# Moving spills and fetches of spectra, and the transposes of normalised rows, around the down projection

## Chip, cores and metric

The kernel runs on one core of a Trainium2 chip. The metric is the device time of one execution in microseconds (us), the median of several runs. The profile is one further execution, recorded by the hardware profiler; its span is a little shorter than the device time, since it starts with the first and ends with the last recorded instruction.

## The reference, cut to what matters

A block of 2048 rows of width 576 goes through an adaptive layer norm with a long causal convolution (part A), and then through another adaptive layer norm with a gated feed-forward network of inner width 4608 (part B). Everything is in bf16.

```python
mod = silu(c) @ w_mod                       # six rows: sa, ca, ga, sb, cb, gb
h = layernorm(q) * (1 + ca) + sa
k_shift = sum over 4 taps of shifted k * shift_k
kv = k_shift * v
y = irfft(rfft(kv padded) * rfft(ssm_k padded))[:S] + kv * ssm_D
x = q + ga * (h * y)
h = layernorm(x) * (1 + cb) + sb
out = x + gb * ((silu(h @ w1) * (h @ w3)) @ w2)
```

## The kernel before, in words

The rows are cut into eight blocks of 256. Part A is a block convolution: for each block s the kernel makes a spectrum X[s] of kv and a spectrum V[s] of the filter, each a tile of 128 x 3456 bf16 (864 KB). The outcome of block s is the sum over j of X[j]*V[s-j], multiplied and added on VectorE (DVE, `pair`, L439 and L441, or L434 for the first term), turned back by matmuls on TensorE (PE, `inverse`, L573), and added to the rows x1 (L587, L588). SBUF holds three X and four V at a time. Older ones are spilled to memory (`keep_x`, L446; `keep_v`, L450) and fetched again when a later block needs them (`get`, L463).

Part B works on pairs of blocks, 512 rows at a time, r = 0 to 3. In the up phase (`stream`, L1018 and L1029; `stream_halves`, L1086, for r = 3) PE multiplies the transposed normalised rows h2T by w1 and w3. In the down phase (`down`, L1143) it multiplies the hidden tile by w2: the output is made in two halves of 288 columns, and each half takes nine pieces of w2 of 288 KB, with 16 matmuls a piece. I number the pieces of one down phase p0 to p17, so p0 to p8 are the first half and p9 to p17 the second. Each piece is loaded by L1132 into one of four buffers, so the load of a piece can be issued when PE has done the piece four before it. These buffers share the memory of the weight tile wst2.

While PE runs row pair r, the convolution of the pair r+1 (blocks 2r+2, even, and 2r+3, odd) runs as a generator beside it: each job and each piece advances the generator by a planned cost (`advance`), and `end()` runs it to its end. Its last steps are, for each of the two blocks, the sums of the layer norm (ScalarE, ACT, L470), its scale (DVE, GpSimd), the normalised rows h2row (ACT, L599), two transposing DMAs from h2row to h2T (`turn_all`, L823), and the scale and shift on the transposed tile (`modulate`, L838 on ACT or L836 on DVE). There is one h2row tile, so the odd block's rows can be written only when the even block's transposes have read it. There are two h2T tiles, for even and odd r.

All these DMAs are issued from SyncE's queue (SP), in one order that the scheduler settles when the program is built: `issue_after(x)` keeps an instruction behind x, and `behind(engine)` behind the newest instruction of that engine. The PSUM pool has four tiles. The down phase's second half holds two of them until DVE has taken them out (`og`, L1168).

In the kernel before, the even block's transposes are issued in the last steps of its own outcome, as soon as its rows are normalised, and are modulated in the next outcome; the odd block's transposes come from `down`, at the eighth piece of the second half (TURN = 7, which is p16), with the modulation behind them. All fetches of old spectra stand behind the last w2 piece of the first half (p8). The spills of X[2] and V[3] stand in the first down phase, that of V[2] in the up phase after it.

Of the kernel before, what the change touches and what calls it, by code (L numbers as in the profile page):

```python
# [24 lines left out]
NRB = S // RB  # L25
FC = 4
NW13 = 3
W2C = 4
# [3 lines left out]
FIRST_DUE = 12.0  # L32
N1 = 24
SPLIT = 2
HEAD = 8
HEAD_PACE = 1.4
AHEAD = 2
EPS = 1e-5
FIRST = (4, 5, 6, 0, 7, 1, 8, 2, 3)
TURN = 7  # L40
QUICK = False


# [6 lines left out]
class _Kernel:  # L50
    def __init__(self, ctx, tc, q, k, v, shift_k, ssm_k, ssm_D, w1, w3, w2, c, w_mod, out):
        self.tc, self.nc = tc, tc.nc
        self.q, self.k, self.v = q, k, v
        self.shift_k, self.ssm_k, self.ssm_D = shift_k, ssm_k, ssm_D
        self.w1, self.w3, self.w2, self.c, self.w_mod, self.out = w1, w3, w2, c, w_mod, out
        pool = lambda name, **kw: ctx.enter_context(tc.tile_pool(name=name, **kw))
        self.const = pool("const", bufs=1)
        self.psum = pool("psum", bufs=4, space=bass.MemoryType.PSUM)
        self.dram = pool("spill", bufs=1, space=bass.MemoryType.DRAM)
        self.spec = pool("spec", bufs=4)  # L60
        self.wprev = pool("wprev", bufs=2)
        self.prod = pool("prod", bufs=1)
        self.acc = pool("acc", bufs=1)
        self.ld = pool("ld", bufs=1)
        self.kvp = pool("kvp", bufs=1)
        self.x1p = pool("x1p", bufs=4)
        self.lnp = pool("lnp", bufs=1)
        self.small = pool("small", bufs=4)
        self.hp = pool("hp", bufs=3)
        self.xo, self.hg, self.accs, self.l1 = {}, {}, {}, {}  # L70
        self.X, self.V, self.Wl = {}, {}, {}
        self.w13, self.kept = {}, {}
        self.last_w2 = None

    def newest(self):
        return self.nc.cur_bb.bb.instructions[-1]
# [382 lines left out]
    def get(self, which, i):  # L459
        t = self.spec.tile([P, 6, D], BF16, name=which, tag=which, bufs=3 if which == "X" else 4)  # L460
        src = self.Xd if which == "X" else self.Vd
        with self.tc.issue_after(self.last_w2) if self.last_w2 is not None else nullcontext():
            self.nc.sync.dma_start(t[:].rearrange("p a d -> p (a d)"), src[i])  # L463
        return t

# [307 lines left out]
    def outcome(self, s, fill, waits, between=None, then=None, quick=False):  # L773


        def steps():
            nc = self.nc
            yield self.real_parts(s)
            yield -waits[0]
            y = self.lnp.tile([P, 2, D], BF16, name="y", tag="y")  # L780
            for cc in range(2):
                nc.scalar.copy(y[:, cc, :].rearrange("p (h d) -> p h d", h=2), self.inverse(s, cc)[:, :, 0:H])
            yield -waits[1]
            self.residual(s, y)
            yield 1.5
            if between is not None:
                between()
            if quick:
                st = []
                for cc in range(2):  # L790
                    st.append(self.quick_stats(self.xo[s][:, cc, :], "l2"))
                    yield 1.25
                for cc in range(2):
                    self.normed(s, cc, *st[cc])
                    yield 0.75
            else:
                sums = [self.small.tile([P, 2], F32, name="l2" + k, tag=t) for k, t in (("s", "ssum"), ("q", "ssq"))]
                for i in range(2):
                    with self.behind(nc.scalar):
                        self.ln_sums(self.xo[s], i, *sums)  # L800
                    yield 0.0
                yield -waits[2] / 2
                if then is not None:
                    then()
                stats = self.ln_var(*sums, "l2")
                yield -waits[2] / 2
                scales = self.ln_shift(*stats)
                yield -3.0
                for cc in range(2):
                    self.normed_act(s, cc, *scales)  # L810
                    yield -1.0
            yield -waits[3]
            self.accs.pop(s)
            self.hg.pop(s)
        yield from self.mix(steps(), fill)

    def turn_all(self, s):

        if s > 1:
            hT = self.h2T[(s // 2) % 2]  # L820
            for cc in range(2):
                t = 2 * (s % 2) + cc
                self.nc.sync.dma_start_transpose(hT[:, :, t * P:(t + 1) * P], self.h2row[:, cc, :])  # L823
            return
        pt = self.ps((P, 2, 1024), BF16)
        for cc in range(2):
            self.turn(pt, cc)
        self.turned(s, pt, 0, 2)

    def modulate(self, s, quick):  # L830

# [30 lines left out]
    def conv(self, s0):  # L862
        s1 = s0 + 1
# [64 lines left out]
        yield from self.mix(self.x_spectrum(s0), beside())  # L928
        yield from self.x_sums(s0)
        yield from self.pair(self.X[s0], V0, s0)  # L930

        def more():
            if not (s0 != 4):
# [2 lines left out]

        def others():
            yield from self.kv_rows(s1)
            self.gate_shift(s1)
            if s0 != 4:  # L940
                yield from self.pair(self.X1, self.V[s0], s1)
            yield from self.mix(self.x_spectrum(s1), more())
            yield from self.x_sums(s1)
        yield from self.outcome(s0, others(), (7.0, 4.5, 6.0, 0.0), lambda: self.gate_rows(s1))
        yield from self.pair(self.X[s1], V0, s1)
        if s1 + 1 < NBLK:
            with self.behind(self.nc.sync):
# [1 line left out]
                self.pair_taps(s1 + 1)  # L949
        yield from self.gate(s1)  # L950
        ahead = self.mix(self.filter_ahead(s1 + 1)) if s1 + 1 < NBLK else ()
        yield from self.outcome(s1, ahead, (5.0, 4.5, 5.0, 0.0), lambda: self.turn_all(s0),
                                lambda: self.modulate(s0, QUICK))

    def filter_ahead(self, s):
        yield -4.0
# [165 lines left out]
    def down(self, r, rate):  # L1122
        nc = self.nc
        for h in range(2):
# [4 lines left out]
            for n, fc in enumerate(FIRST if r == 0 else range(NF // W2C)):  # L1129
                f0 = n * W2C  # L1130
                w = _ap(self.w2m, (h * NF + f0) // W2C % NW2 * W2C * H, [[H, W2C], [1, H]])
                nc.sync.dma_start(w, self.w2[fc * W2C * P:(fc + 1) * W2C * P, h * H:(h + 1) * H]  # L1132
                                  .rearrange("(a p) d -> p a d", p=P))
                last = f0 + W2C == NF
                if h == 0 and last:
                    self.last_w2 = self.newest()
                order = [(f, t) for f in range(W2C) for t in range(4)]
                if f0 == 0:
                    order = [(f, t) for t0 in (0, 2) for f in range(W2C) for t in (t0, t0 + 1)]
                if last:  # L1140
                    order = [(f, t) for t in range(4) for f in range(W2C)]
                for f, t in order:
                    nc.tensor.matmul(acc[t],  # L1143
                                     self.h3[:, fc * W2C + f, t * P:(t + 1) * P], w[:, f, :],
                                     start=(f0 + f == 0), stop=(f0 + f == NF - 1))
                if h == 1 and f0 // W2C == TURN and r + 1 < NRB:

                    self.end()
                    self.turn_all(2 * r + 3)
                    if 2 * r + 5 < NBLK:  # L1150
                        self.pair_taps(2 * r + 5)
                    self.modulate(2 * r + 3, r > 0)
                if (f0 // W2C) % 4 == 3:

                    leave = ((self.keep_v, 3), (), (self.keep_x, 2), (),) if r == 0 else ()
                    for keep, i in filter(None, leave[2 * h + f0 // (4 * W2C):][0:1]):
                        keep(i)
                self.advance(rate * W2C * 4 * 0.126)
            cols = slice(h * H, (h + 1) * H)
            for a in range(2):  # L1160
                s = 2 * r + a
# [41 lines left out]
    def row_blocks(self, n1):  # L1203
        for r in range(NRB):
            cost = 0
            if r + 1 < NRB:
                s0 = 2 * r + 2
# [5 lines left out]
            if r == 0:  # L1213

                jobs = [(fc, 256, 512, None, None) for fc in (n1 - 2, n1 - 1)]

                new = [(n1 + i, 0, RB, b, None) for i, b in enumerate((2, 1, 2))]
                again = [(fc, 256, 512, b, None) for fc, b in enumerate((0, 0, 1, 0))]
                while new or again:
                    jobs += new[0:1] + again[0:1]  # L1220
                    new, again = new[1:], again[1:]
            else:
                spills = {1: (self.keep_x, 1), 2: (self.keep_v, 2), 3: (self.keep_x, 3), 5: (self.keep_v, 0), 6: (self.keep_v, 1)} if r == 1 else {}
                bufs = [b if b == 2 else (r + b) % 2 for b in (0, 1, 2, 0, 1, 2, 0, 1, 0)]
                jobs = [(fc, 0, RB, bufs[fc], (lambda f, i: lambda: f(i))(*spills[fc]) if fc in spills else None)
                        for fc in range(NF // FC)]
# [59 lines left out]
```

## Time and profile before

| | |
|---|---|
| time, median of 3 runs | 504.66 us (504.37 to 505.38) |
| span of the profile | 501.9 us |
| PE busy | 488.2 us, 97% |
| DVE busy | 338.4 us, 67% |
| ACT busy | 282.5 us, 56% |
| DMA queue of SP | 107.4 MB, 71.8% of the 16 DMA engines' span |

The stages can be told apart on PE by the line of its matmuls. The first block and the setup take up to 33 us, the up phase of r = 0 lasts to 122, its down phase to 161, up and down of r = 1 to 277, those of r = 2 to 391, and r = 3 runs to the end. The busy share of an engine over the whole span is a mean over these stages. The profile counts an engine idle before an instruction and names what ended that idle time last[...].

### The profile page before, as it was taken

The numbers are of one execution on the slowest core, as the hardware profiler recorded it, in microseconds if no ns is written. First come the engines' busy times: TensorE is split into PE (matmuls) and PEld (weight loads), VectorE is DVE, ScalarE is ACT, GpSimd is POOL, SyncE is SP. The second block draws the span as 40 slices with busy tenths as digits, with TensorE's granted clock in tenths as the row PEclk, the third lists the DMA queues.
The fourth block names the chain that finished last, engine by engine and source line by source line (L and its number), as shares of the span: only waits on it lengthen the run. The fifth ranks groups of instructions, "written<-read, shape, count | busy, mean of one in ns | idle before, by whom it ended". The sixth has DMA issues, their size and how long they took to land.

```text
span 501.9 us, 8868 instructions
## 1 busy us (share of the span) xinstructions
PE 488.2 (97%) x3528; PEld 286.3 (57%) x3528; DVE 338.4 (67%) x448; ACT 282.5 (56%) x561; POOL 23.0 (5%) x41
## 2 busy tenths in 40 slices
PE   7999999999999999999999999999999999999996
PEld 3667775547776444343777433434777444444774
DVE  8989898898999567997176999699762211111012
ACT  6658679659244688579450456966734355555000
POOL 4200000000001000000000000100000000000000
PEclk9999999999999999999999999999999999999999
DMA  8989986759999878557799897644575454460562
GB/s 281 315 213 235 322 261 204 217 165 313 262 353 304 273 266 247 160 162 223 210 307 340 301 285 247 190 135 148 167 182 136 152 179 148 133 189 1 143 168 67
DMA packets 115037, 107.97 MB, mean 215 GB/s; under 512 B 20340, under 2 KB 107573, under 8 KB 114997
## 3 DMA queue, kind: packets, MB, share of 16 engines
q1 hardware_dynamic: 114974, 107.41, 71.8%
q8 instruction: 27, 0.44, 0.4%
q14 instruction: 14, 0.11, 0.1%
q10 hardware_dynamic: 22, 0.01, 0.0%
HBM read 92.46 MB, written 9.44 MB: 203 GB/s over the span
## 4 chain that ended last, share of the span: by engine, by line
PE 66%; DVE 17%; DMA 8%; ACT 5%; issue 2%; SPq 1%; POOL 0%; POOLq 0%; DVEq 0%; ACTq 0%
PE ps L1018 28%; PE ps L1143 15%; PE ps L1086 14%; PE ps L1029 4%; DMA wst<-in_B_w_dram 4%; DVE p L439 3%; DMA V<-Vd 2%; DVE z L441 2%; ACT junk L470 2%; DVE z L434 2%; DVE og L1168 2%; PE ps L348 2%; DMA kh<-in_A_k_dram 1%; PE ps L573 1%; DVE h L1043 1%
## 5 line engine op out<-in xcount | busy, mean ns | idle before, releaser
L1018 PE MATMUL ps<-h2T,wst 128*128 128x512 bf16 (+1 forms) x1056 | 200.5, 341 | 0.4 <-ACT X L350 0.2
L1018 PEld LDWEIGHTS <-wst 128*128 128x128 bf16 x1056 | 100.1, 98 | 86.7 <-issue 15.0
L1143 PE MATMUL ps<-wst,h 128*128 128x288 bf16 x1152 | 144.9, 286 | 2.2 <-DMA wst<-in_B_w_dram 2.1
L1143 PEld LDWEIGHTS <-h 128*128 128x128 bf16 x1152 | 112.6, 98 | 32.8 <-issue 4.2
L1036 ACT ACTIVATE h<-ps 128x512 bf16<-128x512 f32 x108 | 64.8, 600 | 79.3 <-PE ps L1029 50.3
L1086 PE MATMUL ps<-h2T,wst 64*128 64x512 bf16 x648 | 70.3, 376 | 0.0
L1040 ACT CAST u<-ps 128x512 bf16<-128x512 f32 x108 | 63.3, 586 | 0.0
L439 DVE TENSOR_TENSOR p<-X,V 128x3456 bf16<-128x3456 bf16 x28 | 54.7, 1953 | 4.3 <-DMA V<-Vd 3.9
L441 DVE TENSOR_TENSOR z<-z,p 128x3456 bf16<-128x3456 bf16 x28 | 54.6, 1950 | 0.1
L1086 PEld LDWEIGHTS <-wst 64*128 64x128 bf16 x648 | 31.1, 94 | 38.6 <-DVE og L1168 0.2
L1113 DVE TENSOR_TENSOR h<-h,u 128x1024 bf16<-128x1024 bf16 x18 | 12.5, 692 | 58.1 <-ACT u L1110 58.1
L1043 DVE TENSOR_TENSOR h<-h,u 128x1024 bf16<-128x1024 bf16 x54 | 36.9, 685 | 15.0 <-ACT u L1040 15.0
L1107 ACT ACTIVATE h<-ps 128x512 bf16<-128x512 f32 x36 | 21.5, 597 | 39.8 <-PE ps L1086 39.8
L470 ACT ACTIVATE junk<-x 128x576 bf16<-128x576 bf16 x52 | 35.7, 686 | 3.1 <-DVE x L588 2.6
L1168 DVE TENSOR_TENSOR og<-ps,gbrow 128x576 bf16<-128x576 f32 (+1 forms) x18 | 12.3, 686 | 34.2 <-PE ps L1143 33.6
L1029 PE MATMUL ps<-h2T,wst 64*128 64x512 bf16 (+1 forms) x264 | 33.5, 342 | 0.1
L1110 ACT CAST u<-ps 128x512 bf16<-128x512 f32 x36 | 20.9, 579 | 0.0
L1029 PEld LDWEIGHTS <-wst 64*128 64x128 bf16 x264 | 8.5, 94 | 21.5 <-issue 18.8
L838 ACT ACTIVATE h2T<-h2T,sbcol,cbcol 128x256 bf16<-128x256 bf16 x20 | 10.4, 589 | 16.8 <-DMA h2T<-h2row 16.8
L599 ACT ACTIVATE h2row<-x,l2n,l2r 128x576 bf16<-128x576 bf16 (+1 forms) x24 | 13.8, 654 | 10.2 <-DVE l2n L488 10.2
L368 DVE TENSOR_TENSOR kv<-kv,p 128x1152 bf16<-128x1152 bf16 x24 | 18.1, 753 | 0.3
L362 DVE TENSOR_TENSOR p<-kh,shk 128x3456 bf16<-128x3456 bf16 x8 | 15.6, 1953 | 0.8 <-ACT shk L211 0.6
(135 smaller groups left out, 362.5 us busy)
## 6 DMA issues: line engine op xcount, KB each, us to landing
wst<-in_B_w_dram SPq DMA_DIRECT2D x80, 512.0 KB, 5.1
wst<-in_B_w_dram SPq DMA_DIRECT2D x72, 288.0 KB, 3.4
wst<-in_B_w_dram SPq DMA_DIRECT2D x80, 64.0 KB, 3.3
kh<-in_A_k_dram SPq DMA_DIRECT2D x7, 720.0 KB, 7.0
X<-Xd SPq DMA_DIRECT2D x5, 864.0 KB, 6.8
V<-Vd SPq DMA_DIRECT2D x5, 864.0 KB, 6.0
Xd<-X SPq DMA_DIRECT2D x4, 864.0 KB, 7.7
Vd<-V SPq DMA_DIRECT2D x4, 864.0 KB, 5.5
```

What stands on the lines that cost most here:

```text
L439: nc.vector.tensor_mul(p[:], X[:], V[:])
L441: nc.vector.tensor_add(z[:], z[:], p[:])
L470: self.nc.scalar.activation(junk[:], src[:, i, :], func, scale=scale, accum_out=out[:, col:col + 1])
L1018: nc.tensor.matmul(gus[k][:, i, a * n:(a + 1) * n], w[:, 5 * i + ct, (fi + a) * P:(fi + a + 1) * P], hT[:, ct, t0:t1], start=(first and ct ...
L1029: nc.tensor.matmul(gus[k][:, i, a * n:(a + 1) * n], w[rows, 4, (fi + a) * P:(fi + a + 1) * P], hT[rows, 4, t0:t1], start=(first and a == 0 ...
L1036: nc.scalar.activation(self.h3[:, f:f + m, t0:t1], gus[k][:, 0, :].rearrange("p (a t) -> p a t", a=m), ACT.Silu)
L1040: nc.scalar.copy(self.u[:, k % 2, :], gus[k][:, 1, :])
L1043: nc.vector.tensor_mul(h3, h3, self.u[:].rearrange("p b (a t) -> p (b a) t", a=m))
L1086: nc.tensor.matmul(gus[k][:, i, :], ws[fc][rows, 5 * i + ct if ct < 4 else 4, cols], hT[rows, ct, :], start=swap == 0 and ct == 4, stop=sw ...
L1107: nc.scalar.activation(h3, gus[k][:, 0, :], ACT.Silu)
L1143: nc.tensor.matmul(acc[t], self.h3[:, fc * W2C + f, t * P:(t + 1) * P], w[:, f, :], start=(f0 + f == 0), stop=(f0 + f == NF - 1))
L1168: nc.vector.tensor_mul(g[:, cc, :], ps, _ap(self.gbrow, h * H, [[0, n], [1, H]]))
```

## The change

Four things are changed. The spills of X[2] and V[2] go into the up phase of r = 0, right behind the work that makes them (`keep_v(2)` and `keep_x(2)` in `conv`), instead of the first down phase and the up phase after it. Of the fetches, only the first two (EARLY = 2) that follow a down phase's first half stay behind p8; all later ones stand behind p17. The even block's transposes are held back as `pending`: they are issued at the sixth piece of the second half (EVEN = 5, which is p14), or before the odd block's rows are normalised if that comes earlier, and modulated at p16 (MOD = 7). The odd block's transposes move from p16 to p17 (TURN = 8) and stand behind the newest SP instruction, the load of p17. The purpose is to keep other transfers out of the way of the w2 pieces in the down phases.

```diff
--- before.py
+++ after.py
@@ -32,12 +32,13 @@
 FIRST_DUE = 12.0
 N1 = 24
 SPLIT = 2
+EARLY = 2
 HEAD = 8
 HEAD_PACE = 1.4
 AHEAD = 2
 EPS = 1e-5
 FIRST = (4, 5, 6, 0, 7, 1, 8, 2, 3)
-TURN = 7
+EVEN, MOD, TURN = 5,7,8
 QUICK = False
 
 
@@ -70,7 +71,8 @@
         self.xo, self.hg, self.accs, self.l1 = {}, {}, {}, {}
         self.X, self.V, self.Wl = {}, {}, {}
         self.w13, self.kept = {}, {}
-        self.last_w2 = None
+        self.last_w2 = self.late_w2 = self.pending = self.raw = None
+        self.fetched = 0
 
     def newest(self):
         return self.nc.cur_bb.bb.instructions[-1]
@@ -459,7 +461,9 @@
     def get(self, which, i):
         t = self.spec.tile([P, 6, D], BF16, name=which, tag=which, bufs=3 if which == "X" else 4)
         src = self.Xd if which == "X" else self.Vd
-        with self.tc.issue_after(self.last_w2) if self.last_w2 is not None else nullcontext():
+        self.fetched += 1
+        behind = self.last_w2 if self.fetched <= EARLY else self.late_w2
+        with self.tc.issue_after(behind) if behind is not None else nullcontext():
             self.nc.sync.dma_start(t[:].rearrange("p a d -> p (a d)"), src[i])
         return t
 
@@ -806,9 +810,12 @@
                 yield -waits[2] / 2
                 scales = self.ln_shift(*stats)
                 yield -3.0
+                self.turn_pending()
                 for cc in range(2):
                     self.normed_act(s, cc, *scales)
                     yield -1.0
+                if s % 2 == 0:
+                    self.pending = s
             yield -waits[3]
             self.accs.pop(s)
             self.hg.pop(s)
@@ -826,6 +833,12 @@
         for cc in range(2):
             self.turn(pt, cc)
         self.turned(s, pt, 0, 2)
+
+    def turn_pending(self):
+        if self.pending is not None:
+            with self.behind(self.nc.sync):
+                self.turn_all(self.pending)
+            self.raw, self.pending = self.pending, None
 
     def modulate(self, s, quick):
 
@@ -928,6 +941,8 @@
         yield from self.mix(self.x_spectrum(s0), beside())
         yield from self.x_sums(s0)
         yield from self.pair(self.X[s0], V0, s0)
+        if s0 == 2:
+            self.keep_v(2)
 
         def more():
             if not (s0 != 4):
@@ -936,6 +951,8 @@
 
         def others():
             yield from self.kv_rows(s1)
+            if s0 == 2:
+                self.keep_x(2)
             self.gate_shift(s1)
             if s0 != 4:
                 yield from self.pair(self.X1, self.V[s0], s1)
@@ -949,8 +966,7 @@
                 self.pair_taps(s1 + 1)
         yield from self.gate(s1)
         ahead = self.mix(self.filter_ahead(s1 + 1)) if s1 + 1 < NBLK else ()
-        yield from self.outcome(s1, ahead, (5.0, 4.5, 5.0, 0.0), lambda: self.turn_all(s0),
-                                lambda: self.modulate(s0, QUICK))
+        yield from self.outcome(s1, ahead, (5.0, 4.5, 5.0, 0.0))
 
     def filter_ahead(self, s):
         yield -4.0
@@ -1134,6 +1150,9 @@
                 last = f0 + W2C == NF
                 if h == 0 and last:
                     self.last_w2 = self.newest()
+                    self.fetched = 0
+                if h == 1 and f0 // W2C == 8:
+                    self.late_w2 = self.newest()
                 order = [(f, t) for f in range(W2C) for t in range(4)]
                 if f0 == 0:
                     order = [(f, t) for t0 in (0, 2) for f in range(W2C) for t in (t0, t0 + 1)]
@@ -1143,16 +1162,21 @@
                     nc.tensor.matmul(acc[t],
                                      self.h3[:, fc * W2C + f, t * P:(t + 1) * P], w[:, f, :],
                                      start=(f0 + f == 0), stop=(f0 + f == NF - 1))
+                if h == 1 and f0 // W2C == EVEN and r + 1 < NRB:
+                    self.turn_pending()
+                if h == 1 and f0 // W2C == MOD and r + 1 < NRB:
+                    self.modulate(self.raw, QUICK)
                 if h == 1 and f0 // W2C == TURN and r + 1 < NRB:
 
                     self.end()
-                    self.turn_all(2 * r + 3)
+                    with self.behind(nc.sync):
+                        self.turn_all(2 * r + 3)
                     if 2 * r + 5 < NBLK:
                         self.pair_taps(2 * r + 5)
                     self.modulate(2 * r + 3, r > 0)
                 if (f0 // W2C) % 4 == 3:
 
-                    leave = ((self.keep_v, 3), (), (self.keep_x, 2), (),) if r == 0 else ()
+                    leave = ((self.keep_v, 3), (), (), (),) if r == 0 else ()
                     for keep, i in filter(None, leave[2 * h + f0 // (4 * W2C):][0:1]):
                         keep(i)
                 self.advance(rate * W2C * 4 * 0.126)
@@ -1220,7 +1244,7 @@
                     jobs += new[0:1] + again[0:1]
                     new, again = new[1:], again[1:]
             else:
-                spills = {1: (self.keep_x, 1), 2: (self.keep_v, 2), 3: (self.keep_x, 3), 5: (self.keep_v, 0), 6: (self.keep_v, 1)} if r == 1 else {}
+                spills = {1: (self.keep_x, 1), 3: (self.keep_x, 3), 5: (self.keep_v, 0), 6: (self.keep_v, 1)} if r == 1 else {}
                 bufs = [b if b == 2 else (r + b) % 2 for b in (0, 1, 2, 0, 1, 2, 0, 1, 0)]
                 jobs = [(fc, 0, RB, bufs[fc], (lambda f, i: lambda: f(i))(*spills[fc]) if fc in spills else None)
                         for fc in range(NF // FC)]
```

## The prediction

> **What bounds the kernel now.** I read the page's busy times first, then PE's waits, then busy time by stage, and then, at the ends of the down phases, the chain that ended last and SyncE's (SP) own timeline. PE is busy 97% of the span, and the order of its instructions as built is the same before and after the change. So the change can only move the time by PE's idle time. PE's waits (us in total, times, longest):
>
> ```profile
> PE ps L1143 <- DMA wst<-in_B_w_dram: 2.1, 5, 0.9
> ```
>
> All waits of PE for w2 together are 2.1 us. Busy time by stage (window, length, then busy us of PE, PEld, DVE, ACT, POOL, clock, DMA share, GB/s), for down and up phases in turn:
>
> ```profile
> 122.00:161.00 39.00, 38.11 (x307) 29.71 (x305) 36.85 (x41) 17.56 (x36) 2.96 (x2) 1.00 1.10 308
> 161.00:238.00 77.00, 77.00 (x390) 31.59 (x389) 60.07 (x75) 58.14 (x118) 2.51 (x3) 1.00 0.73 226
> 238.00:277.00 39.00, 38.10 (x308) 29.92 (x306) 20.74 (x27) 12.41 (x25) 0.69 (x1) 1.00 0.93 286
> 277.00:354.00 77.00, 76.94 (x388) 31.47 (x387) 72.81 (x76) 50.52 (x100) 1.38 (x2) 1.00 0.66 209
> 354.00:391.00 37.00, 36.72 (x300) 29.10 (x298) 18.40 (x32) 17.86 (x37) 1.80 (x2) 1.00 0.65 175
> ```
>
> The up phases have no PE idle time worth naming; the three down phases idle 0.89, 0.90 and 0.28 us, with the DMA engines full in the first two. PE's timeline shows whose data it waited for: p6, p14 and p16 of the first, p15 of the second, p17 of the third.
>
> ```profile
> 133.97 2.12 PE L1143 MATMUL ps<-wst,h 128*128 128x288 bf16 x16 [0.27 <-DMA wst<-in_B_w_dram]
> 156.65 4.08 PE L1143 MATMUL ps<-wst,h 128*128 128x288 bf16 x32 [0.45 <-DMA wst<-in_B_w_dram]
> 270.91 6.04 PE L1143 MATMUL ps<-wst,h 128*128 128x288 bf16 x48 [0.90 <-DMA wst<-in_B_w_dram]
> ```
>
> SP's timeline gives the reason: p6 (issued at 129.07) stood behind the even rows' transposes, p16 (150.34) behind a fetch.
>
> ```profile
> 126.35 2.62 SPq L823 DMA_TRANSPOSE h2T<-h2row  x2
> 129.07 0.54 SPq L1132 DMA_DIRECT2D wst<-in_B_w_dram  x1
> ...
> 149.01 1.24 SPq L463 DMA_DIRECT2D X<-Xd  x1
> 150.34 0.39 SPq L1132 DMA_DIRECT2D wst<-in_B_w_dram  x1
> ```
>
> The chain that ended last holds a second limit, at the end of the second down phase:
>
> ```profile
> 266.91 6.93 DMA V<-Vd
> ...
> 273.93 1.97 DVE p L439
> ...
> 282.57 0.76 DVE og L1168
> 283.33 0.04 issue
> 283.37 0.41 PE ps L348 x2
> ```
>
> The fetch of a V lands, DVE works through products and two `og` evacuations behind it, and PE's first filter matmul of the next up phase starts 0.04 us after the second `og`. So this fetch is already exactly on time: what it loses, PE loses.
>
> [...] SP stands 15.3 us in total at L823 for h2row, and what is queued behind stands too. [...] p16, behind the 864 KB fetch, landed 6.27 us after its issue (the chain's 150.34 to 156.61), where the median of w2 pieces is 3.4; p6, behind two transposes, took 4.86. [...]
>
> **The change part by part.** The built SP order gives the positions; times below are from the trace before, less stalls removed.
>
> *Spills earlier.* X[2] is finished by DVE at 92.6 (L384 at 91.86, 0.76 long). SP would have issued wst2's loads from 88.4; behind the spill it does from 92.7. PE uses wst2 at 102.98, and a 512 KB load lands in 5.1: hidden by 5 us. V[2] is ready by then. Cost 0; gain: 0.86 MB of some 12 MB less in the first down phase, at 308 GB/s 2.8 us of transfer.
>
> *First down phase.* The even transposes leave p6: gain 0.27. They now stand between p14 and p15, whose issue moves to 148.9 from 148.4; with 4.86 to land that is 153.8 against a use at 153.5: 0 to 0.5 lost. The fetch of X[0] goes ahead of p12 (issue about 141.5, landing like p16's 6.27 at 147.8, use at 147.6): 0.2 lost for the 0.45 gained. The 0.17 at p14 I count as gained. New is a wait: the taps' transposing load (L304), which before came behind the phase (160.39), now stands ahead of p17, and it must wait until the copies to kT (L313) have read the taps' tile. These are issued up to 150.4; a copy lands in 3.9 (median), 5.9 in this stage. So SP stands until 154.3 to 156.3, spends 1.3 on the transpose and issues p17 at 155.7 to 157.7, where its use is due at 157.4. With 3.4 to 4.9 to land, p17 starts at 159.1 to 162.6. The odd transposes queue behind it: 2.6 of issue and 2.6 to 3.2 to land from the last issue's start, so the tile is there about 4.5 after p17's issue, and ACT's five modulations (0.51 apart) let PE start 1.6 later, at 161.8 to 163.8, where before it was 160.57. Loss 1.2 to 3.2 less what is uncertain in the waits; I take 1.6, with 0 and 3.5 as ends.
>
> *Second down phase.* p11 is issued at 257.03 as before; the even transposes follow it (2.6), so p12 goes out at 260.3 instead of 258.3. It lands 4.86 later, at 265.2, and PE wants it at 264.0: 1.2 lost. V[2]'s fetch goes ahead of p13 (landing 261.5 + 6.27 = 267.8, wanted at 267.2): 0.6 lost. Gained: the 0.90 at p15. p17's load follows p13's end at 269.8, the odd transposes 2.6 later, and the third fetch, the V that the chain above shows, starts at 273 instead of 266.91. A V fetch right behind a transpose took 4.70 in this stage (250.36 to 255.06), others up to 6.93: it lands at 277.7 (to 280) instead of 273.84. In the new DVE order the second `og` ends 7.5 behind the start of that product (two products of 1.97 and 1.87, one sum of 1.87, two `og` of 0.75, one L1169 of 0.37), not 9.4 as before. So PE's filter matmul is released at 285.2, where before it was 283.37: 1.8 lost. If the w2 pieces don't stall, p17 goes out at 268.4 and all is 1.4 earlier: 283.8, 0.4 lost; with 6.93 for the fetch 2.2 more. Ends -0.5 and 3.5.
>
> *The next up phase.* DVE runs its chain some 4.4 later, PE 1.8. DVE's slack before: kv for block 6 is done at 311.05 and PE takes it at 317.11 (6.0); the even outcome's tile at 341.5 against 344.4 (2.9, behind 3.7 of idle DVE). The difference of 2.6 fits. Cost 0.
>
> *Third down phase.* p17 no longer stands behind the odd transposes: 0.28 gained. The even transposes between p14 and p15 cost p15 0 to 0.5. The odd rows' chain (rows normalised at 384.5, transposes, modulation ending at 388.7) ends 2.4 before the up phase: hidden. Net -0.1.
>
> Sum: +1.6 +1.8 -0.1 = +3.3, less 0.2 for the lighter queues: 507.8.
>
> **Rivals.** (1) Relief wins: the w2 waits vanish and nothing takes their place. This is worth at most 0.27+0.17+0.45+0.90+0.28 = 2.1, giving 502.6. For it speaks that the DMA engines are full in these stages; against it, that the same transposes and fetches stay in the phase, only at other pieces. (2) Relief and new waits cancel, as when kT's copies land in 2.1 (their shortest) and the late V in 4.7 without stalls ahead: 0 to +0.4, or 504.7. For it speaks the latency's spread, against it the `og` with 0.04 us of slack. (3) Both waits at their upper ends: 3.5 + 3.5 - 0.3 = 6.7, some of it hidden by PE's own lateness: 510.5.
>
> **How the numbers follow.** Forecast 0.48; (1) 0.20; (2) 0.17; (3) 0.15. Faster by over 0.2% (below 503.65) is (1) with a little of (2): 0.21. Same: 0.17. Slower: forecast and (3), 0.62. The range leaves out the lower part of (1) and the upper of (3): 503.0 to 510.6.
>
> **What would show it.** Right: in the first down phase PE waits for p17 or for the first up matmul (L1018), SP waits at L304 for L313's copies; in the second, waits at p12 or p13, and an `og` that ends at 284 or later with a PE wait at L348 or L1018 behind it; the late V issued behind L823 near 272. Wrong: L304 issued without a wait, p17 landing by 158, and the `og` still before PE. The largest doubt is how long transfers take to land in a queue that is less full.

## The result and the profile after

The changed kernel takes 508.40 us (505.89 to 511.63), where the kernel before took 504.99 in the same comparison. The ratio is 1.0062, interval 1.0044 to 1.0080: slower by 3.4 us. The profiled execution has a span of 507.0 us, against 501.9.

PE is busy for 489.0 us, as before, so the loss lies in its idle time and, as will be seen, in its clock. PE's waits between 120 and 470 us of the changed kernel (us in total, times, longest):

```profile
PE ps L1162 <- DMA wst<-in_B_w_dram: 2.3, 2, 1.2
PE ps L350 <- DVE og L1192: 2.0, 1, 2.0
```

The waits for w2 did not shrink. They were five of at most 0.9 us and are now two of 1.2 and 1.1. A wait for `og` has come on top. By stage (window, length, busy us of PE, PEld, DVE, ACT, POOL, clock, DMA share, GB/s):

```profile
122.00:161.00 39.00, 37.82 (x309) 29.96 (x307) 36.39 (x40) 16.51 (x34) 2.95 (x2) 1.00 0.99 274
161.00:238.00 77.00, 76.65 (x388) 31.21 (x385) 59.78 (x74) 58.32 (x119) 2.50 (x3) 1.00 0.69 217
238.00:277.00 39.00, 37.91 (x302) 29.32 (x301) 17.80 (x22) 13.88 (x29) 0.69 (x1) 1.00 0.85 221
277.00:354.00 77.00, 74.97 (x375) 30.87 (x373) 71.72 (x77) 47.26 (x95) 1.38 (x2) 0.98 0.72 242
354.00:391.00 37.00, 37.00 (x286) 27.47 (x285) 21.86 (x30) 19.79 (x42) 1.80 (x2) 1.00 0.60 156
```

The down phases do move less: their rates were 308, 286 and 175 GB/s and are 274, 221 and 156. The third has lost its 0.28 us of PE idle time. But PE idles 1.18 in the first and 1.09 in the second, and the up phase behind the second, which had nothing to lose before, has 2.03 us of idle time and a mean clock of 0.98. PE's timeline names the places (start, us, instruction, in brackets the idle time ahead of it and what ended it):

```profile
159.29 2.12 PE L1162 MATMUL ps<-wst,h 128*128 128x288 bf16 x16 [1.18 <-DMA wst<-in_B_w_dram]
161.25 2.72 PE L1034 MATMUL ps<-h2T,wst 128*128 128x512 bf16 x8
...
268.69 9.96 PE L1162 MATMUL ps<-wst,h 128*128 128x288 bf16 x80 [1.09 <-DMA wst<-in_B_w_dram]
...
287.05 0.41 PE L350 MATMUL ps<-kT,Fk 128*128 128x288 bf16 x2 [2.03 <-DVE og L1192]
```

The first is p17 of the first down phase. The next line is the start of the up phase: eight matmuls take 2.72 us, where the same eight took 1.89 in the kernel before, because the odd rows' tile is modulated late (ACT begins it at 160.60 and takes 2.57 for its five parts). The third is p13 of the second down phase, and the last is the filter matmul that needs a PSUM tile back from `og`. SP's timeline shows why p17 was late:

```profile
154.38 1.30 SPq L306 DMA_TRANSPOSE knat<-in_A_ssm_k_dram  x1
155.77 0.53 SPq L1148 DMA_DIRECT2D wst<-in_B_w_dram  x1
```

The taps' transposing load now stands ahead of p17. SP waited there for the copies to kT, which must have read the tile first:

```profile
SPq L306 <- DMA kT<-knat: 1.9, 1, 1.9
```

DVE's timeline shows why `og` was late:

```profile
279.60 1.96 DVE L441 TENSOR_TENSOR p<-X,V 128x3456 bf16<-128x3456 bf16 x1 [1.37 <-DMA V<-Vd]
281.47 0.75 DVE L1192 TENSOR_TENSOR og<-ps,gbrow 128x576 bf16<-128x576 f32 x1
...
286.24 0.75 DVE L1192 TENSOR_TENSOR og<-ps,gbrow 128x576 bf16<-128x576 f32 x1
```

The product at 279.60 waits for the V whose fetch was issued at 273.94, behind the odd transposes. DVE ran its instructions in the order built, so both `og` wait with it, the second until 286.24, though the last matmul of the down phase had ended by 278.65.

Between the starts of the stages, after less before: +0.74 us up to the first down phase, which the runs described below vary by as much; +0.77 for the first down phase and the up phase behind it; +0.19 for the second down phase; +3.66 for the up phase behind that; -0.31 for the third down phase. The third up phase holds 2.0 us of waiting for `og` and 1.7 more, in which the same matmuls simply took longer: from 287.83 on, for 3.41 us, a clock of only 0.50 was granted to PE. This is one execution of each kernel; the medians lie 3.4 apart. Of the 20 executions of the changed kernel, nine have a mean granted clock of 0.998 or more. One such stretch would alone bring it down to 0.9966 (half of 3.41 us in a span of 507.0), so that part of the loss is not in every execution.

### The profile page after: what moved, and what is told of

It reads as the page before. It is cut to its first block, busy times and chain, and to the rows that moved or that the text cites. A ratio compares the mean times of both kernels' runs of the same rounds, so it can differ in the third digit from the quotient of the medians.

```text
span 507.0 us, 8871 instructions
## 1 busy us (share of the span) xinstructions
PE 489.0 (96%) x3528; PEld 290.8 (57%) x3528; DVE 339.0 (67%) x448; ACT 282.3 (56%) x561; POOL 22.9 (5%) x41
## 4 chain that ended last, share of the span: by engine, by line
PE 71%; DVE 13%; DMA 6%; ACT 5%; SPq 2%; issue 2%; POOL 0%; DVEq 0%; ACTq 0%
PE ps L1034 27%; PE ps L1162 21%; PE ps L1102 14%; PE ps L1045 4%; DMA wst<-in_B_w_dram 2%; PE ps L350 2%; DVE p L441 2%; ACT junk L474 2%; DVE z L443 1%; PE ps L577 1%; DMA kh<-in_A_k_dram 1%; DVE h L1059 1%; SPq L830 1%; DVE kv L370 1%; DVE p L364 1%
## 5 line engine op out<-in xcount | busy, mean ns | idle before, releaser
L1034 PE MATMUL ps<-h2T,wst 128*128 128x512 bf16 (+1 forms) x1056 | 202.6, 342 | 1.1 <-DMA wst<-in_B_w_dram 0.3
L1102 PEld LDWEIGHTS <-wst 64*128 64x128 bf16 x648 | 36.1, 94 | 33.8 <-PE ps L1162 0.4
L1045 PEld LDWEIGHTS <-wst 64*128 64x128 bf16 x264 | 8.5, 94 | 21.5 <-issue 20.5
L352 ACT CAST W<-ps 128x576 bf16<-128x576 f32 x12 | 7.6, 646 | 20.8 <-PE ps L350 18.6
L436 DVE TENSOR_TENSOR z<-X,V 128x3456 bf16<-128x3456 bf16 x7 | 13.7, 1954 | 4.1 <-DMA V<-Vd 3.0
```

What stands on the lines that cost most here:

```text
L1034: nc.tensor.matmul(gus[k][:, i, a * n:(a + 1) * n], w[:, 5 * i + ct, (fi + a) * P:(fi + a + 1) * P], hT[:, ct, t0:t1], start=(first and ct ...
L1045: nc.tensor.matmul(gus[k][:, i, a * n:(a + 1) * n], w[rows, 4, (fi + a) * P:(fi + a + 1) * P], hT[rows, 4, t0:t1], start=(first and a == 0 ...
L1102: nc.tensor.matmul(gus[k][:, i, :], ws[fc][rows, 5 * i + ct if ct < 4 else 4, cols], hT[rows, ct, :], start=swap == 0 and ct == 4, stop=sw ...
```

## The experiments

The runs fall into four comparisons of their own, in which the kernel before took 505.32, 505.47, 504.98 and 505.12 us. Ratios are to it. The changed kernel was not measured again in them: it stands at 1.0062 of the kernel before, from the result above.

**E1, fetches between the pieces again.**

```diff
-EARLY = 2
+EARLY = 99
```

> Undoes one part: all fetches stand behind p8 again, as before the change; spills, transposes and their waits stay as changed. My theory: the late fetch of V[3] (issued at 273.9 in the changed kernel) holds the second og, and PE waited 2.0 us for it and then ran about 4 us at half clock; with the fetch issued near 268 that wait is gone, and the w2 pieces behind the fetches lose up to 0.9 again: 505.5, between 504.6 and 506.5. Rival (the loss lies in the transposes and the taps' load alone): 508, as changed.

It took 508.98 us (ratio 1.0067, 1.0044 to 1.0090): no gain, against my expectation. The wait for `og` was gone. In its place PE waited for w2 in three places, 3.7 us in total. Two of these, 0.89 before the last eighty matmuls of the second down phase and 1.67 at its p17, stand where the fetches are back between the pieces. So the late fetches do bring something; what they cost elsewhere is as large.

**E2, og first.** The products with late-fetched spectra are ordered behind `og` on DVE. No transfer of the down phase is moved; from 279 us on, in the up phase behind it, the scheduler also set some issues of SP anew.

```diff
-        nc.vector.tensor_mul(p[:], X[:], V[:])
+        late = self.fetched > EARLY and self.last_og is not None
+        with self.tc.issue_after(self.last_og) if late else nullcontext():
+            nc.vector.tensor_mul(p[:], X[:], V[:])
...
+                    self.last_og = self.newest()
```

> Keeps every DMA of the second down phase where the change put it, and only orders the products that use late fetches behind the two og of the second half on DVE. My theory (the cost is that og stands behind a product that waits for the fetch): og ends near 280, no PE wait at the first filter matmul and no half clock: 3.0 to 3.7 us less in the profile, 505.0 between 504.3 and 506.0. Rival (the bunched transfers after p17 are what slows PE, by way of its weights): 508, as changed.

It took 506.60 us (1.0023, 1.0006 to 1.0039), a little outside the range. In DVE's timeline, `og` comes ahead of the product again:

```profile
281.76 0.76 DVE L1194 TENSOR_TENSOR og<-ps,gbrow 128x576 bf16<-128x576 f32 x1
282.43 1.95 DVE L443 TENSOR_TENSOR p<-X,V 128x3456 bf16<-128x3456 bf16 x1
```

PE's wait at the filter matmul and the slow stretch behind it are gone. From the start of the second down phase to that of the third it is 116.3 us, against 119.6 in the changed kernel and 115.8 before. The median gained only 1.8 of these 3.4: in the recorded execution the first and the third down phases were 0.9 and 0.8 us longer than in the changed kernel, and PE waited 3.1 us for w2 instead of 2.3. By the ratios, which take out the difference of the comparisons, E2 gained 2.0.

**E3, the taps' load behind.** One SP instruction, L306 for the sixth taps, goes behind the odd transposes.

```diff
-                if s1 + 1 < NBLK:
+                if s1 + 1 < NBLK and s0 == 2:
                     self.load_taps(s1 + 1)
+            if s1 + 1 < NBLK and s0 > 2:
+                with self.tc.issue_after(self.late_w2):
+                    self.load_taps(s1 + 1)
```

> Moves one SP instruction: the taps' transposing load of the first down phase stands behind the odd transposes instead of ahead of p17's load; nothing else moves. My theory: p17 goes out near 152.5 instead of 155.8, PE's 1.18 wait for it is gone, and the odd transposes are bound by the normalised rows: 0.8 to 1.3 less, 507.3. Rival (p17 is late because of the even transposes and the fetch ahead of it, or the odd rows themselves are late): under 0.3 less, 508.2.

It took 506.77 us (1.0027, 1.0007 to 1.0046), somewhat faster than I expected. The 1.18 us wait for p17 was gone and the first down phase 0.9 shorter; the wait for `og` stayed, at 2.32. The eight matmuls at the start of the up phase still took 2.71, so L306 is not all that makes them slow. Nor is it p17's load here. SP had issued that by 153.20 and then stood for the odd block's rows:

```profile
152.12 1.08 SPq L1151 DMA_DIRECT2D wst<-in_B_w_dram  x2
155.71 2.53 SPq L830 DMA_TRANSPOSE h2T<-h2row  x2
```

ACT made these rows only from 154.50 on, behind three modulations of the even tile, which had to wait for the even transposes until 153.01. So in this trace it is the later place of the even block that makes the odd tile late.

**E4, even transposes at once.**

```diff
                 if s % 2 == 0:
-                    self.pending = s
+                    self.turn_all(s)
+                    self.raw = s
```

> Undoes one part: the even block's transposes are issued as soon as its rows are normalised, as before the change; the modulation stays at p16, fetches and spills as changed. My theory: p12 of the second down phase no longer waits (1.09), p17 and the late fetch come about 1.1 earlier, so the og too: 1.0 to 2.0 less there, p6 of the first down phase loses 0.3 again and p17 of it gains up to 0.5: 507.0, between 506.0 and 507.8. Rival (the even transposes' place costs nothing, since og decides alone): 508.4.

It took 509.57 us (1.0088, 1.0058 to 1.0118). The wait in the second down phase went, as expected, and that stage was 38.03 us, against 38.69. The first down phase lost more: it grew from 38.73 to 40.27, with waits of 0.98, 0.56 and 0.86. The wait of 0.98 is for a piece whose load stood behind the even transposes (issued from 124.74). The wait of 0.86 is for p16: the scheduler now put L306 (at 153.04) ahead of p16 and p17 both. In return the next up phase had no slow start: its first eight matmuls took 1.89. With the set piece the stage was thus shorter in the first down phase and longer in the second, but in the first L306 moved as well, so what the even transposes' place is worth there is not shown.

**E5, og first and taps behind.** The edits of E2 and E3.

> Both single edits together: the products of late-fetched spectra behind og on VectorE, and the sixth taps' transposing load behind the odd transposes on SyncE. Alone they took 1.8 and 1.6 us off the changed kernel in one and the same comparison. Theory (two separate losses, one in each down phase): they add, 508.4 - 1.8 - 1.6 = 505.0, range 504.3 to 506.0; the first w2 wait before the second up phase and the wait for og before the third are both gone and no half clock is granted near 287. Rival A (the down phases share one budget of transfers, so that what leaves one place is paid at another): little more than one of them, 506.0 to 506.8. Rival B (the fetches behind the last w2 piece save something of their own once their two side effects are gone): under 504.3.

It took 504.65 us (0.9974, 0.9957 to 0.9990). The two losses add: alone the edits took 0.39% and 0.35% off the ratio of 1.0062, together 0.88%. That is the whole loss, and a little more.

**E8, PE kept busy.** Fourteen dummy matmuls at the end of the second down phase.

```diff
+            if r == 1 and h == 1:
+                for _ in range(14):
+                    nc.tensor.matmul(accs[1][:, 1, H:512], self.ident[:], self.h3[:, 0, 0:512 - H],
+                                     start=True, stop=True)
```

> The changed kernel with fourteen dummy matmuls of 224 columns, whose output nobody reads, between the last matmul of the second down phase and the filter matmul that waits for og. They fill about 1.3 us of that 2.0 us wait and move nothing else before it. Theory (the half clock of 4 us is granted because TensorE stood still for 2 us; it is a second loss of 1.7 us on top of the wait): the wait ends at the same time, some 0.7 us of it left empty, no half clock near 287, and 508.4 - 1.7 = 506.7, range 506.0 to 507.3. Rival (the clock falls for another reason, such as what the other engines do just then): the half clock stays and the time is 508.4, range 507.8 to 509.5.

They ran at 279.0, ahead of the first up matmuls, which were 1.35 us later for it. So it is PE's arrival at the wait that was moved, not a part of the wait that was filled. `og` let PE go at 287.75, after 0.88 us of idle time instead of 2.03. The granted clock of the changed kernel in one window of 1 us (columns as above, the clock third from the end), and below it the same window with the dummy matmuls:

```profile
288.00:289.00 1.00, 1.00 (x4) 0.41 (x3) 1.00 (x2) 0.13 (x1) 0.00 (x0) 0.50 0.98 378
288.00:289.00 1.00, 1.00 (x7) 0.48 (x5) 1.00 (x1) 0.64 (x1) 0.00 (x0) 1.00 0.97 380
```

Four matmuls a microsecond became seven. From the filter matmul to the third down phase it is 70.70 us instead of 72.39: 1.69 saved, the size I gave the slow clock. The median, 507.88 (1.0050, 1.0032 to 1.0068), missed my range and can't be told from the changed kernel's: the dummies' own 1.35 us and a wait for p13 of 1.32 instead of 1.09 stand against the saving. So in this one trace the half clock went when the wait was shortened; the time does not show it. Of its 22 executions, 14 have a mean clock of 0.998 or more, against nine of 20 of the changed kernel. That points the same way, but is no proof.

**E6, the spills alone**, on the kernel before.

```diff
+        if s0 == 2:
+            self.keep_v(2)
...
+            if s0 == 2:
+                self.keep_x(2)
...
-leave = ((self.keep_v, 3), (), (self.keep_x, 2), (),) if r == 0 else ()
+leave = ((self.keep_v, 3), (), (), (),) if r == 0 else ()
...
-spills = {1: (self.keep_x, 1), 2: (self.keep_v, 2), 3: (self.keep_x, 3), ...
+spills = {1: (self.keep_x, 1), 3: (self.keep_x, 3), ...
```

> The kernel before with the spills alone moved: V[2] and X[2] go to memory in the second up phase, as in the changed kernel; fetches and transposes are those of before. Theory (my prediction's step: spills in the down phases cost nothing, as they land beside w2 pieces that are loaded three ahead): 505.0, 504.4 to 505.6. Rival (the spills took transfer time from the w2 pieces of the first down phase, so that this part of the change is a gain hidden under the losses of the others): 503.5 to 504.4. Rival B (in the up phase they delay weight loads): 505.6 to 507.

It took 507.22 us (1.0031, 1.0013 to 1.0048): this part alone is a loss of 1.75 us, which neither of my two main cases had. The spills went out at 79.8 and 92.5, in the up phase of r = 0, as meant. SP's timeline near the end of the first down phase:

```profile
152.19 1.30 SPq L304 DMA_TRANSPOSE knat<-in_A_ssm_k_dram  x1
153.59 1.08 SPq L1136 DMA_DIRECT2D wst<-in_B_w_dram  x2
```

The taps' load, at 160.39 in the kernel before, has moved ahead of p16 and p17, waits 4.3 us for the copies to kT there, and PE then waits 1.79 for p16. Nobody edited this load: with the spills gone the fetch of X[0] went out at 140.65 instead of 149.01, and the scheduler set the rest anew.

**E9, the spills and the taps' load behind**, on the kernel before (the edits of E6 and E3).

> The kernel before with the spills moved, as in the run of the spills alone, and the sixth taps' transposing load held behind the last w2 piece again. That run lost 1.75 us, and in its trace the sixth taps' load had come ahead of two w2 pieces on SyncE and waited 4.3 us there. Theory (the transfers of the spills cost nothing, it is the order on SyncE, which the planner makes anew when they go, that costs): the loss is gone, 505.0 to 505.5 where before has 505.5, and the w2 wait of 1.8 us near 157.7 is gone. Rival (the spills in the up phase themselves cost it): 506.8 to 507.5. Rival B (without the spills the first down phase is shorter than before): 504.0 to 504.9.

It took 505.67 us (1.0006, 0.9985 to 1.0027), no difference from before. The wait for p16 is gone in its trace. Yet the stage is no shorter there, 40.12 us against 40.10 in E6, as w2 waits of 0.45, 0.96 and 0.57 stand earlier in it. By time the theory holds; since the intervals of E6 and E9 overlap, E9 alone would not settle it.

**E11, the taps' load moved alone**, on the kernel before. Two added orders, without a wait, put the sixth taps' load just ahead of p17 and keep the second odd transpose behind p17; no other instruction changes place.

```diff
+                if s0 == 4:
+                    self.tc.add_manual_dep(
+                        self.late_w2, self.newest().name,
+                        mybir.DependencyInfo(mybir.DependencyClass.NoSync, mybir.DependencyReason.DATA),
+                        reason="taps ahead")
+                    self.tc.add_manual_dep(
+                        self.second, self.late_w2.name,
...
```

> The kernel before with a single instruction moved: the sixth taps' transposing load (L304) stands between the two odd transposes, just ahead of the load of the last w2 piece of the first down phase, instead of behind the phase; spills, fetches and all other orders are those of before. Theory (the place of this one load costs, with or without the spills): SP issues it near 155, the last piece goes out some 1.3 to 2 us later than before's 155.07 and lands 3.4 to 4.9 later, at 160 to 162, where PE was ready at 158.6: 1.2 to 3 us slower than before, 506.2 to 508. Rival (the order on SP is not what cost in the run of the spills alone, but the spills' own transfers or the fetch that went ahead): within 0.5 of before.

It took 507.00 us (1.0037, 1.0019 to 1.0056): one DMA moved costs 1.9 us. Its trace on SP:

```profile
157.33 1.28 SPq L304 DMA_TRANSPOSE knat<-in_A_ssm_k_dram  x1
158.67 0.58 SPq L1141 DMA_DIRECT2D wst<-in_B_w_dram  x1
```

and on PE, p17:

```profile
162.71 2.12 PE L1154 MATMUL ps<-wst,h 128*128 128x288 bf16 x16 [1.46 <-DMA wst<-in_B_w_dram]
```

No wait for kT is needed: SP stood at the odd transposes until 155.95 anyway. The load's 1.28 us of issue stands ahead of the last piece. The load of p17 went out 3.60 later than in the kernel before, of which 2.19 are older: SP came to the odd transposes that much later. PE had also waited in this trace at four earlier pieces, 0.40 to 0.75 each, whose loads were issued ahead of the moved one, so not all that is longer in it is the edit's doing.

**E7, even transposes of the second down phase at once**, on top of E5. The first down phase keeps the set piece. The edit moves those of the third down phase, too (issued from 362.9 on instead of 379.1).

```diff
-                if s % 2 == 0:
+                if s == 2:
                     self.pending = s
+                elif s % 2 == 0:
+                    self.turn_all(s)
+                    self.raw = s
```

> The run with both edits, and the even block's transposes of the second down phase issued at once instead of at their set piece (the first down phase keeps the set piece, where it helped). Theory (the set piece's transposes make the next w2 piece 1.1 us late in the second down phase, and issuing all at once there took that wait away and made that stage about 0.4 us shorter than the run with the taps' edit): 504.6, 0.2 to 0.6 under the run with both edits. Rival (the time comes back at the next wait of the stage, as it did in the first down phase): 505 or more, not under the run with both edits.

It took 502.94 us (0.9967, 0.9949 to 0.9986), faster than the kernel before and the lowest median of all, 1.7 below E5, where I had expected 0.2 to 0.6. In its trace no wait of 0.25 us or more is left on PE from 107 us on, and the second down phase (these are its own bounds) has none:

```profile
238.52:276.12 37.60, 37.60 (x306) 29.73 (x305) 18.35 (x26) 12.40 (x25) 0.69 (x1) 1.00 0.98 263
```

Against E5 the ratios do not separate the two (0.9967 and 0.9974); what differs in the traces is E5's wait of 1.08 for p13.

**E10, E7 with fetches between the pieces** (EARLY = 99).

> The fastest version so far (og first, taps behind, even transposes of the second down phase at once) with its fetches between the w2 pieces again, as before the change. Theory (fetches behind the last w2 piece are worth their place once their products no longer stand ahead of og: with them between the pieces, w2 waits of 1 to 2 us come back in the second down phase): 504.5, 503.5 to 506.0. Rival (the gain of that version over the kernel before comes from spills and transposes alone): no slower than it, 502.7 to 503.4.

With EARLY = 99 no fetch counts as late, so the order of E2 lapses too; no wait of PE for `og` stands in the trace. It took 505.08 us (1.0001, 0.9982 to 1.0019). A wait of 1.19 for w2 is back in the second down phase:

```profile
273.98 2.12 PE L1170 MATMUL ps<-wst,h 128*128 128x288 bf16 x16 [1.19 <-DMA wst<-in_B_w_dram]
```

The late fetches are thus worth about 1.7 us (0.34% of 505) once nothing is lost by them. The intervals overlap a little, but the second down phase alone is 1.6 longer here (39.24 us instead of 37.60).

**E12, E7 with the spills back** where they were before.

> The fastest version (og first, taps behind, even transposes of the second down phase at once) with the spills where they were in the kernel before. Theory (my prediction's step that spills are worth nothing either way, once the orders on SP are kept): 502.9 to 503.9, no measurable difference from the fastest version's 0.9967 of before. Rival (the spills out of the first down phase carry a good part of the gain, since 0.86 MB less is moved there): 504.0 to 505.5, w2 waits in the first down phase are back.

It took 504.51 us (0.9983, 0.9964 to 1.0002), between the two cases. One wait for p17 of the first down phase, 0.74, is back in its trace. Whether the spills' own place is worth something stays open: the ratios differ by 0.16%, less than the width of either interval.

## Why the prediction was right, step by step

Direction and size were right: 507.8 was forecast, +3.1 on 504.66, and +3.4 on 504.99 was measured. The steps fared unequally.

- *Spills earlier, cost 0.* Wrong as a statement on this part. Their transfers cost nothing that E9 can show, but moving them makes the scheduler set SP's order anew, and E6 alone lost 1.75 us. I had read the new order from the build and charged it, correctly, to the first down phase; I had not seen that the spills' move alone is enough to bring it.
- *First down phase, 1.6 lost.* Right in mechanism, too large in the recorded execution. SP waited at L306 for the copies to kT until 154.38 (I had 154.3 to 156.3), p17 went out at 155.77 (155.7 to 157.7) and started at 159.29 (159.1 to 162.6). But my times counted from the trace before, and this phase began 0.74 later; less that, all three lie 0.5 to 0.7 below my lower ends. Undoing that one order gained 1.6 us (E3), imposing it alone on the kernel before cost 1.9 (E11). The trace shows only 0.77 for the stage and the next, as earlier w2 waits of 0.9 vanished beside it. The late odd tile is a part I had as well, but only one of its sources: in the changed kernel the odd transposes stand behind p17, yet without L306 ahead they wait for the odd rows (E3), and the slow start stays 0.55 us large in E7 (2.44 instead of 1.89). I had not asked what the even block's later place does to the odd block.
- *Second down phase, waits at p12 and p13.* Half right: none at p12, 1.09 at p13, where I had 1.2 and 0.6. p13's load is issued behind the fetch and took 5.67 to land; I had taken 6.27.
- *The late V and `og`, 1.8 lost.* Right in mechanism. The fetch was issued at 273.94 (I had 273, for a phase that began 1.5 earlier) and took 5.56 to land, where I took 4.70, the lower of my two values; `og` ended 7.4 behind the product's start (7.5). PE waited 2.03. E2 removes it with every transfer of the down phase left in place, so it is the order on DVE, not the place of the fetch alone, that must be blamed.
- *The next up phase, cost 0.* Wrong. In the recorded execution it lost 1.7 us to a clock of 0.50 for 3.41 us, 0.8 us behind the end of the wait, that I had not foreseen.
- *Third down phase, -0.1.* Right: -0.31, the wait for p17 gone.

Rival 1, relief wins, and rival 2, both cancel, fell as the changed kernel stands; E5 and E7 show that they fell by two orders, one on SP and one on DVE. Rival 3, both waits at their upper ends, fell by its size. In the recorded execution the sum is 4.3 us without what comes ahead of the first down phase: 2.6 of longer waits and late tiles, where I had 3.3, and 1.7 of half clock, where I had nothing. Over all executions the clock counts for less. By their mean clocks I estimate that the changed kernel lost 1.9 us a run to it (20 executions) and the kernel before 1.2 (50 executions, first comparison), a difference of 0.7. So that the forecast came within 0.3 us was partly luck: the clock is missing from it, and some of its waits are too large.

## What to carry to other kernels

Moving the fetches out of the busy stage was worth about 1.7 us here (E10 against E7). Moving the spills alone made the scheduler set SP's order anew and cost 1.75 (E6). So compare the whole order before and after, and ask of each instruction that changed place what it waits for and what stands behind it, also of those that nobody edited. A product whose input was made later on purpose should not stand ahead of an evacuation on the same engine: in the changed kernel DVE ran both in the order built, waited 1.37 us for the fetch of V, and PE waited 2.03 for the second `og`. Giving the evacuation precedence cost nothing here (E2, a ratio of 1.0023 instead of 1.0062). And a position that suits one round of a loop need not suit the next: the version with the lowest median has the even transposes in two places. That the set piece is the better one in the first down phase is not shown, since E4 moved a second load there.

## What the runs showed of the hardware

In three traces a wait of TensorE of over 2 us was followed by a stretch at half the clock. In the changed kernel, E3 and E4 the wait was 2.03, 2.32 and 2.34 us, and each time a clock of 0.50 was granted for 3.4 us, beginning 0.1 to 1.0 us behind the wait. Half the clock for 3.4 us is a loss of 1.7. After waits of 1.67 (E1), 1.79 (E6) and 0.88 us (E8) the clock stayed at 1.00.

The length of a wait does not decide alone. Six traces (E1, E2, E3, E5, E7, E11) hold such a stretch between 26 and 32 us as well, with no wait over 1.3 us in the 10 us ahead. In E5 (busy PE is the second number):

```profile
25.00:26.00 1.00, 1.00 (x15) 0.74 (x16) 0.96 (x3) 0.00 (x0) 0.00 (x0) 1.00 0.95 358
26.00:27.00 1.00, 1.00 (x15) 0.82 (x14) 0.93 (x4) 0.00 (x0) 0.20 (x1) 0.84 1.05 380
27.00:28.00 1.00, 1.00 (x10) 0.67 (x8) 0.97 (x3) 0.10 (x2) 0.36 (x1) 0.50 1.06 340
28.00:29.00 1.00, 1.00 (x6) 0.62 (x5) 0.97 (x4) 0.16 (x3) 0.00 (x0) 0.50 1.08 301
29.00:30.00 1.00, 1.00 (x7) 0.72 (x6) 0.34 (x2) 0.68 (x2) 0.55 (x1) 0.50 1.10 338
30.00:31.00 1.00, 0.83 (x10) 0.56 (x8) 0.86 (x3) 1.00 (x3) 0.00 (x0) 0.95 1.09 306
```

From 23.11 on PE ran sixty matmuls of only 64 columns there, without idle time. In the kernel before, the changed kernel, E4, E6 and E8 the same matmuls run at that place, and the clock stays at 1.00. What sets the granted clock is not shown by these runs.

In the kernel before, the transposing DMAs held SP's queue longer than the plain load of a w2 piece: their issue took SP 1.2 to 1.3 us at L823 and 1.3 to 3.1 at L304, where a w2 piece took 0.37 (median; 1.18 at most).
